# Sparse attention into a gated feed-forward layer: batch 0's last matrix product in seven products, with its neighbours moved

## The chip, the cores and the metric

The kernel runs on one core of one Trainium2 chip. The metric is the device time of one execution in microseconds (us), as the median of several runs. TensorE (PE) does the matmuls, and its weight loads are listed apart as PEld. VectorE (DVE), ScalarE (ACT) and GpSimd (POOL) do the rest of the arithmetic; SyncE (SP), POOL and ACT issue transfers. Each engine works through its own queue in order.

## The reference

```python
def _attn_ref(q, k, v):                  # 4 batches, 8 heads, 768 tokens, 64 per head
    k_sum = k.reshape(B, H, nb, block, D).max(axis=3)        # block = 32, nb = 24
    v_sum = v.reshape(B, H, nb, block, D).mean(axis=3)
    scores_l = scale * q @ k.T           # kept only where |i - j| < 16
    scores_s = scale * q @ k_sum.T + log(block)
    a = softmax(concat([scores_l_masked, scores_s]))
    return a @ concat([v, v_sum])

def _moe_ref(x, w_in, w_out):            # x: 3072 x 512, w_in: 512 x 2048, w_out: 2048 x 512
    h = x @ w_in
    g = h * (1.0 / (1.0 + np.exp(-1.702 * h)))
    return (g @ w_out).astype(np.float32)
```
Each query sees its near neighbours (31 keys at most) and one row for each block of 32: the maximum of the keys, the mean of the values. The result of the attention goes through two matrix products with a gelu between them.

## The kernel before

The four batches run one after the other; a batch's 768 tokens are two halves of 384. The feed-forward layer of one batch runs on PE while the attention of the next batch (or of the same batch's other half, in batch 0) is slipped between its matmuls. All instructions are kept in the order in which the program writes them, on each engine.

Attention of one half, for four pairs of heads p: `scores` (24 narrow matmuls into a two-bank PSUM tile, then an exp on ACT), `mask` (a multiplication on DVE), `values` (48 narrow matmuls for two pairs, then a `norm` on DVE for each), `tx` (six transposes on PE for two pairs and a copy to `xTT`). In batches 2 and 3 a DMA transpose (`dx`) takes the place of `tx`. Before that, queries and keys must stand transposed: batch 0's late queries through `q_late` (PE turn, DVE copy), batch 1's through `tk` and `tq`, those of later batches through the DMA transposes `xk` and `xq`. The rows for the value blocks come from `vsum` (48 narrow matmuls), `block_sums` (DVE) and `sum_dmas`; `halo_dmas` copy the neighbours' rows. `value_rows` is all four.

Feed-forward: an ff tile (`ff_in`, `ff_one`, `ff_open`) is four matmuls of 384 columns into one bank and a gelu on ACT, which writes 128 of the 2048 inner columns of a half into `gT`; 16 tiles make a half. The second product is done in two ways:

- plain (`ff_out`): for a tile of 128 tokens 16 matmuls of 512 columns, in four parts of four. Batch 0 does all six tiles so.
- in seven products (`product`): two tiles of tokens, left and right, and two halves of w_out are combined as in Winograd's form of Strassen's product, so that seven products of eight matmuls with 256 columns give what eight would give otherwise. It needs the sums `ws` of w_out (`w_sum`, once) and the sums `gs` of gT (`g_sums`), and between the products copies (`keep_it`) and additions (`give`) that read the PSUM banks. Batches 1 to 3 do this.

PSUM's eight banks are two pools: `pmm`, four tiles of one bank, and `psb`, two tiles of two banks. A new tile takes the bank that is free first in program order and waits for the last reader of the one before.

What runs between which matmuls is written out by hand: `plan0` (batch 0's second half between its own first half's `ff_out`), `plan1` (batch 1 between batch 0's second `ff_out`), `plan` (batches 2 and 3 between the products of the batch before) and `todo` (work between the second half's ff tiles). An entry such as "s02" means scores, half 0, pair 2; "m" mask, "v" values, "x" turn back, "t" and "q" queries, "d" DMA transpose, "R" the value rows, "g" the gelu table. ACT holds one table at a time, so `exp_soon` and `gelu_soon` load the next one ahead of its first use.

Loads go through POOL's queue in the order of `load_batch`: for batches 1 to 3 keys, values, queries (batch 3's queries later, gated by a small copy that waits for a transfer). Behind them on POOL stand the halo copies of batch 1's keys.

Of the kernel before, what the change touches and what calls it, by code (L numbers as in the profile page):

```python
# [35 lines left out]
def kernel(  # L36
# [295 lines left out]
    def vrows0():  # L332

        dve.tensor_copy(out=gate3[:, 1:2], in_=gate3[:, 0:1])
# [227 lines left out]
    def tq(p, s, eng):  # L562
        ps = pmm.tile([128, 1024], BF16, name="ps_t", tag="mm")[:, 0:S]
# [37 lines left out]
    def values(b, half, g):  # L601

        if b == 1:
# [27 lines left out]
    def tx(half, g):  # L631
        ps = psb.tile([128, 2, HALF], F16, name="ps_x", tag="big")
# [4 lines left out]
        dve.tensor_copy(out=xTT[half][g], in_=ps)  # L637
# [17 lines left out]
    def ff_in(half, nts):  # L655

        phs = [pmm.tile([128, HALF], F32, name="ph", tag="mm") for nt in nts]
# [25 lines left out]
    def g_sums(j, eng=dve, which=(0, 1, 2, 3)):  # L683
# [91 lines left out]
    def product(b, t, what):  # L775
        n = NT // 2
        l = slice(t * 128, t * 128 + 128)
        r = slice(HALF + t * 128, HALF + t * 128 + 128)
        lo, hi = slice(0, N1), slice(N1, d_model)
        raw_l, raw_r = gTb[:, :, l], gTb[:, :, r]  # L780
# [18 lines left out]
        def keep_it(name):  # L799
# [4 lines left out]
            copy(dve if t == 0 and b + 1 < B else act, t_, po)  # L804
# [20 lines left out]
        elif what == 2:  # L825
            give("o1", lo, "s1")
            if last:
                store("o1", t * 128, lo)
# [4 lines left out]
        elif what == 7:  # L833
            give("o2", hi, "s5")
            if last:
                store("o2", HALF + t * 128, hi)
        elif what == 3:
            give("o1", hi, "s2")
            store("o1", t * 128, hi if last else slice(0, d_model))
        elif last:  # L840
            give("o2", lo, None)
            store("o2", HALF + t * 128, lo, act)
        else:
            give("o2", lo, None)
            store("o2", HALF + t * 128)
# [410 lines left out]
```

## Time and profile before

| | |
|---|---|
| median of 3 runs | 206.43 us (206.40 to 206.73) |
| the profiled execution | 205.39 us, its span 203.4 us |
| PE busy | 196.7 us, 97% of the span |
| PEld, DVE, ACT, POOL busy | 136.6, 141.2, 125.4, 89.9 us |
| plain matmuls `po` | 96 |
| matmuls of products in batches 1 to 3 | 504 of 256 columns |
| table loads on ACT | 10 of 1.28 us |
| granted clock of PE | 0.998 of full speed |

The span is the time from the first instruction to the last in the profile. Stages on PE: batch 0's first half of attention up to 20.6 us, its first half's ff tiles up to 30.7, `ff_out` with the second half's attention up to 44.8, the second half's ff tiles up to 57.2, `ff_out` with batch 1's attention up to 74.8, batch 1's ff tiles up to 96.6, its products with batch 2's attention up to 119.0, and the same again for batch 2; batch 3 has no attention beside it. Nearly all instructions are recorded at one line, L28, the wrapper that keeps the order; so they are told apart by the names of their tiles.

### The profile page before, as it was taken

Reading aid. Unit: us, or ns where it says so; the run is one execution under the profiler, and the core shown is the slowest. Engines: PE = TensorE matmul, PEld = TensorE weight load, DVE = VectorE, ACT = ScalarE, POOL = GpSimd, SP = SyncE. Lnnn points to the kernel's source line nnn. Section 1 sums busy time; section 2 is a strip of 40 time slices with the busy share of each in tenths; the row PEclk is TensorE's granted clock in tenths of the full one; section 3 lists DMA queues with packets and bytes.
Section 4 is the critical chain, followed back from the end, with each engine's and each line's share of the span. In section 5 each row is a group of like instructions: output and inputs, shape, how many; then the busy total and the mean of one; then the engine's idle time right before and its main releaser. Section 6 shows DMA issues by size and latency. Waiting matters only on the chain.

```text
span 203.4 us, 5851 instructions
## 1 busy us (share of the span) xinstructions
PE 196.7 (97%) x2358; PEld 136.6 (67%) x2358; DVE 141.2 (69%) x391; ACT 125.4 (62%) x240; POOL 89.9 (44%) x141
## 2 busy tenths in 40 slices
PE   6889999999999999999999999999999999999993
PEld 5548655556754566655888876666888865578882
DVE  6586894694856884898767789896769567758221
ACT  4584976638786717777871446778670559984220
POOL 7964489447899584000986034000000009980000
PEclk9999999999999999999999999999999999999999
DMA  5999999999999999999999979999022930000223
GB/s 171 169 165 204 207 207 215 189 156 243 116 122 170 176 170 178 127 165 155 114 181 156 173 140 139 110 247 179 0 104 62 185 119 3 0 0 0 106 105 103
DMA packets 95994, 28.13 MB, mean 138 GB/s; under 512 B 83664, under 2 KB 93152, under 8 KB 95968
## 3 DMA queue, kind: packets, MB, share of 16 engines
q0 software_dynamic: 69648, 13.24, 84.8%
q1 hardware_dynamic: 26176, 14.39, 34.8%
q8 instruction: 18, 0.29, 0.6%
q10 hardware_dynamic: 144, 0.13, 0.2%
q14 instruction: 8, 0.07, 0.1%
HBM read 27.26 MB, written 6.29 MB: 165 GB/s over the span
## 4 chain that ended last, share of the span: by engine, by line
PE 91%; DMA 3%; DVE 3%; issue 1%; ACT 0%; POOLq 0%; DVEq 0%
PE ph L28 32%; PE poA L28 16%; PE po L28 11%; PE poB L28 7%; PE phA L28 4%; PE ps_av L28 4%; PE poC L28 4%; PE ps_s L28 3%; DMA qe<-in_q_dram 3%; DVE ks L28 2%; PE ps_t L28 1%; PE ps_x L28 1%; PE phC L28 1%; PE phB L28 1%; PE phE L28 1%; DVE qT L28 1%
## 5 line engine op out<-in xcount | busy, mean ns | idle before, releaser
L28 PE MATMUL ph<-xT,w_in_sb 128*128 128x384 f16 x400 | 67.8, 326 | 0.1
L28 PEld LDWEIGHTS <-w_in_sb 128*128 128x128 f16 x442 | 42.7, 98 | 27.2 <-issue 0.2
L28 ACT ACTIVATE gT<-ph 128x384 f16<-128x384 f32 x100 | 47.9, 491 | 18.4 <-PE ph L28 17.6
L28 PEld LDWEIGHTS <-gT 128*128 128x128 f16 x312 | 28.8, 98 | 11.3 <-issue 0.2
L28 ACT ACTIVATE a_sb<-ps_s 128x768 bf16<-128x768 f32 (+1 forms) x32 | 25.0, 826 | 12.0 <-PE ps_s L28 12.0
L28 PEld LDWEIGHTS <-gs 128*128 128x128 f16 x288 | 27.7, 98 | 3.4
L28 POOL DMA_DIRECT2D vw<-in_v_dram x36 | 24.6, 699 | 11.9 <-DMA kb<-in_k_dram 5.4
L28 POOL TENSOR_TENSOR gs<-gT 128x384 f16<-128x384 f16 x8 | 7.3, 911 | 43.3 <-ACT gT L28 43.2
L28 PE MATMUL po<-w_out_sb,gT 128*128 128x512 f16 x96 | 23.6, 380 | 0.0
L28 PE MATMUL poA<-ws,gs 128*128 128x256 f16 x144 | 18.7, 273 | 0.0
L28 DVE TENSOR_TENSOR a_sb<-a_sb,mk 128x768 bf16<-128x768 bf16 x28 | 14.9, 554 | 5.5 <-ACT a_sb L28 5.0
L28 DVE TENSOR_TENSOR x<-ps_av,rc 128x384 f16<-128x384 f32 x32 | 17.8, 557 | 1.1
L28 DVE TENSOR_TENSOR gs<-gT 128x384 f16<-128x384 f16 (+1 forms) x34 | 13.3, 390 | 7.2 <-ACT gT L28 6.9
L28 POOL DMA_DIRECT2D qb<-in_q_dram x16 | 15.1, 961 | 2.5 <-DMA w_in_sb<-in_moe_w_in_dram 1.2
L28 PEld LDWEIGHTS <-kx 64*128 64x128 bf16 (+1 forms) x378 | 9.9, 95 | 6.8 <-issue 3.6
L28 POOL DMA_DIRECT2D kb<-in_k_dram x14 | 13.6, 986 | 0.3 <-issue 0.3
L28 DVE TENSOR_REDUCE ks<-kx 128x24 bf16<-128x768 bf16 x12 | 11.4, 948 | 3.4 <-ACT kx L28 3.2
L28 ACT ACT_TABLE_LOAD x10 | 12.8, 1283 | 1.0 <-PEq L1240 0.8
L28 ACT ACTIVATE osb<-poA 128x256 f32<-128x256 f32 x9 | 3.5, 384 | 16.1 <-PE poA L28 16.1
L28 ACT ACTIVATE s<-poA 128x256 f32<-128x256 f32 x11 | 4.2, 385 | 11.2 <-PE poA L28 11.2
L28 PEld LDWEIGHTS <-a_sb 128*64 128x64 bf16 (+2 forms) x400 | 7.9, 108 | 2.8 <-issue 1.3
L28 PE MATMUL poA<-ws,gT 128*128 128x256 f16 x72 | 9.3, 273 | 0.0
(117 smaller groups left out, 288.2 us busy)
## 6 DMA issues: line engine op xcount, KB each, us to landing
out_dram<-osb SPq DMA_DIRECT2D x22, 256.0 KB, 3.9
kb<-in_k_dram POOLq DMA_DIRECT2D x14, 192.0 KB, 6.6
qb<-in_q_dram POOLq DMA_DIRECT2D x12, 192.0 KB, 10.5
vw<-in_v_dram POOLq DMA_DIRECT2D x36, 64.0 KB, 5.5
w_out_sb<-in_moe_w_out_dram POOLq DMA_DIRECT2D x4, 512.0 KB, 12.8
w_in_sb<-in_moe_w_in_dram POOLq DMA_DIRECT2D x3, 512.0 KB, 12.4
vw<-vs SPq DMA_DIRECT2D x6, 198.0 KB, 6.6
gT<-in_k_dram SPq DMA_DIRECT2D x2, 384.0 KB, 3.4
```

Source lines behind the costliest of these rows:

```text
L28: r = f(*a, **kw)
```

## The change

Batch 0 does two tiles plainly (tokens 0 to 255) and the other four in two groups of seven products (`seq0`), with the left tile of a group in columns 256 and 512 of gT and the right one 128 further. Of the two plain tiles three quarters stand between the second half's attention, and the last quarter behind the first four ff tiles of the second half, which take two banks of each pool. The two groups of products stand where the second half's `ff_out` stood, with batch 1's attention between them.

With that: two of batch 0's late query loads are issued ahead of the first quarter of w_out, and two of the late query turns stand ahead of the last ff tile; batch 0's block rows (`vrows0`) come ahead of the key work; all sums of w_out stand together at the start of the second half's ff tiles; new sums over gT (`g_sums0`, four inner tiles and 256 columns at a time) between and behind these tiles; batch 1's value rows go behind product (0,2). The turns back go through ACT, and most of them through one-bank tiles. Masks 2 and 3 of batch 0's second half stand between two norms. In batch 0's products the copies of group 0 go through ACT. In batches 1 and 2 the matmuls over the next batch's value rows stand behind the last ff tiles and the block sums behind product (0,1); batch 2's queries are loaded ahead of its values, batch 3's queries with its keys and its values later; the query transposes are issued at the third pair of ff tiles in both.

```diff
     def load_batch(b):
...
+        load_turned(q, b, qb2, "qb", (0,) if b == 1 else (0, 1))
+        if b < 3:
+            load_v(b)
         if b == 1:
-            load_turned(q, b, qb2, "qb", (0,))
-        load_v(b)
-        if b < 3:
-            load_turned(q, b, qb2, "qb", (1,) if b == 1 else (0, 1))
+            load_turned(q, b, qb2, "qb", (1,))
...
     def vsum(s):
-        if s == 1 and not vs_ps[0]:
-            ps = [pmm.tile([128, 512], F32, name="ps_vs", tag="mm") for e in range(2)]
-        else:
-            big = psb.tile([128, 1024], F32, name="ps_vs", tag="big")
-            ps = [big[:, 0:512], big[:, 512:1024]]
+        ps = [pmm.tile([128, 512], F32, name="ps_vs", tag="mm") for e in range(2)]
...
     def vrows0():
-        dve.tensor_copy(out=gate3[:, 1:2], in_=gate3[:, 0:1])
...
-    def values(b, half, g):
+    def values(b, half, g, mm=False, between=()):
...
             norm(...)
+            if i == 0:
+                for p in between:
+                    mask(half, p)
...
-    def tx(half, g):
+    def tx(half, g, eng=dve, mm=False):
...
-        dve.tensor_copy(out=xTT[half][g], in_=ps)
+        copy(eng, xTT[half][g], ps)
...
+    def g_sums0(j0, j1, which, eng=dve):
+        def pairs(n0):
+            a = gTb[:, n0 + j0:n0 + j1, HALF - 128:S].rearrange("p j (a i c) -> p j a i c", i=2, c=128)
+            return a[:, :, :, 0], a[:, :, :, 1]
+        (l1, r1), (l2, r2) = pairs(0), pairs(NT // 2)
+        o = [gs[:, w, j0:j1, 0:256].rearrange("p j (a c) -> p j a c", c=128) for w in range(4)]
+        for w in which:
+            a, b_, op = {0: (r1, r2, ALU.add), 1: (o[0], l1, ALU.subtract),
+                         2: (l1, r1, ALU.subtract), 3: (l2, o[1], ALU.subtract)}[w]
+            eng.tensor_tensor(out=o[w], in0=a, in1=b_, op=op)
...
     def product(b, t, what):
-        r = slice(HALF + t * 128, HALF + t * 128 + 128)
+        tok_l, tok_r = (t * 128, HALF + t * 128) if b else (HALF - 128 + t * 256, HALF + t * 256)
...
-            copy(dve if t == 0 and b + 1 < B else act, t_, po)
+            copy(dve if t == 0 and 0 < b and b + 1 < B else act, t_, po)
...
+    seq0 = [(0, 1), (0, 2), (0, 5), (1, 1), (0, 6), (0, 7), (0, 3), (0, 4),
+            (1, 2), (1, 5), (1, 6), (1, 7), (1, 3), (1, 4)]
...
+    for a in range(2):
+        load_q1(a)
     load_w_out(0)
-    for a in range(NP):
+    for a in range(2, NP):
         load_q1(a)
...
     halo_dmas(w50, JH)
+    vrows0()
...
-    plan0 = {1: ["q0", "q1", "q2"], 2: ["s0", "s1", "q3", "m0", "m1"], 4: ["s2", "s3", "m2", "m3"], 6: ["v0", "v1"], 8: ["x0"], 9: ["x1"]}
-    plan1 = {-1: ["s00", "s01"], 1: ["t2", "m00", "m01"], 2: ["t3", "s02"], 3: ["s03", "m02"], 4: ["m03", "s10"],
-             5: ["s11", "m10"], 6: ["v00", "m11", "s12", "s13"], 7: ["v01", "g"], 8: ["m12", "m13"],
-             9: ["x00", "x01", "v10"], 10: ["v11"], 11: ["x10"]}
+    plan0 = {-1: ["s0", "s1"], 0: ["q2"], 1: ["m0", "q3", "m1", "s2", "s3", "v0"],
+             3: ["v1", "x0"], 5: ["x1"]}
+    plan1 = {1: ["R"], 2: ["s00", "s01"], 4: ["t2", "t3", "m00", "m01"], 5: ["s10", "s11"],
+             6: ["m10", "m11"], 7: ["s02", "s03"], 8: ["m02", "m03"], 9: ["s12", "s13"],
+             10: ["m12", "v00", "g"], 11: ["v01"], 12: ["x00", "v10"], 13: ["x01", "v11"]}
...
     for nt in range(N0, NT):
         ff_in(0, (nt,))
-        if nt == 12:
-            act.activation(out=gate3[:, 0:1], in_=gate[:, 0:1], func=ACT.Copy)
-            vrows0()
+        if nt == 14:
+            for p in range(2):
+                q_late(p, dve)
...
-    for i, (ms, part) in enumerate((ms, part) for part in range(4) for ms in range(JH)):
+    for i, (ms, part) in enumerate((ms, part) for part in range(3) for ms in range(2)):
         ff_out(0, ms, part)
         beside0(i)
...
-    ff_in(1, range(3))
-    for nt in range(3, NT):
-        ff_in(1, (nt,))
+    for what, part in ((0, 0), (0, 1), (1, 0), (1, 1), (2, 0), (2, 1), (3, 0), (3, 1)):
+        w_sum(what, part)
...
+    ff_in(1, order2[0:4], 2)
+    for ms in range(2):
+        ff_out(0, ms, 3)
...
-    beside(1, -1)
-    for i, (ms, part) in enumerate((ms, part) for ms in range(JH) for part in range(4)):
-        ff_out(1, ms, part)
+    for i, (t, what) in enumerate(seq0):
+        product(0, t, what)
+        if i == 0:
+            g_sums0(4, NT // 2, (0, 1))
+        if i == 2:
+            g_sums0(4, NT // 2, (2, 3))
         beside(1, i)
-        if i == 2:
+        if i == 4:
             load_batch(2)
...
             if n == 0:
-                ff_open(order2[0:4], (lambda: tx(1, 1)) if b == 1 else None)
+                ff_open(order2[0:4], (lambda: tx(1, 0, act)) if b == 1 else None)
+                if b == 1:
+                    tx(1, 1)
+                    for nt in order2[4:6]:
+                        ff_one(0, nt)
...
                 if n == 0 and b > 1:
-                    load_turned(q, b + 1, qb2, "qb")
-                if n // 2 == 1:
-                    value_rows(s)
-                if n // 2 == 2 * b:
+                    load_v(b + 1)
+                if n // 2 == 7:
+                    halo_dmas(vw[s].rearrange("p (j e) h c -> p j e h c", e=2), 0)
+                    vsum(s)
+                if n // 2 == 2:
                     xq(0, s)
                     xq(1, s)
...
             product(b, t, what)
             if i == 0:
+                if nxt:
+                    block_sums()
+                    sum_dmas(vw[s].rearrange("p (j e) h c -> p j e h c", e=2), 0)
                 g_sums(NT // 2 - 1, dve, (2, 3))
```

More of the change, by code (lines that the diff above doesn't have):

```diff
@@ L560, in tk, with tq @@
         rest_k(p, s, pool)
-    def tq(p, s, eng):
-        ps = pmm.tile([128, 1024], BF16, name="ps_t", tag="mm")[:, 0:S]
+    def tq(p, s, eng, big=False):
+        ps = (psb.tile([128, 2048], BF16, name="ps_t", tag="big") if big
+              else pmm.tile([128, 1024], BF16, name="ps_t", tag="mm"))[:, 0:S]
         turn_tiles(ps, qb2[p // 2][:, p % 2], NJ)
@@ L629, in norm @@
                        rc.to_broadcast([128, 2, JH, D]))
-    def tx(half, g):
-        ps = psb.tile([128, 2, HALF], F16, name="ps_x", tag="big")
+    def tx(half, g, eng=dve, mm=False):
+        ps = (pmm if mm else psb).tile([128, 2, HALF], F16, name="ps_x", tag="mm" if mm else "big")
         for i in range(2):
@@ L653, in ff_step, with ff_in @@
                       rhs=xTT[half][g][:, i], start=(n == 0), stop=(n == KO - 1))
-    def ff_in(half, nts):
-        phs = [pmm.tile([128, HALF], F32, name="ph", tag="mm") for nt in nts]
+    def ff_in(half, nts, n_mm=4):
+        phs = [pmm.tile([128, HALF], F32, name="ph", tag="mm") if i < n_mm
+               else psb.tile([128, 1024], F32, name="ph", tag="big")[:, 0:HALF] for i in range(len(nts))]
         for part in ((0, 1), (2, 3)):
@@ L827, in product @@
             if last:
-                store("o1", t * 128, lo)
+                store("o1", tok_l, lo)
         elif what == 6:
@@ L1051, in beside0 @@
             elif what[0] == "v":
-                values(0, 1, i)
+                values(0, 1, i, i == 0, (2, 3) if i == 0 else ())
             else:
-                tx(1, i)
+                tx(1, i, act)
     def beside(b, slot):
@@ L1059, in beside @@
             if what[0] == "t":
-                tq(i, 1, dve)
+                tq(i, 1, dve, True)
             elif what[0] == "m":
@@ L1069, in beside @@
             elif what[0] == "v":
-                values(b, half, i)
+                first_ = b == 1 and half == i == 0
+                values(b, half, i, first_)
+                if first_:
+                    mask(1, 3)
             elif what[0] == "d":
@@ L1073, in beside @@
             else:
-                tx(half, i)
+                tx(half, i, act, True)
     def value_rows(s):
@@ L1138 @@
                 for nt in order2[n:n + 2]:
-                    for half in range(2):
+                    for half in range(int(b == 1 and n == 4), 2):
                         ff_one(half, nt)
```

33 lines of the change are left out of this document (17 added, 16 removed).

## The prediction

> **What bounds the kernel now.** I read the page first, then the busy time of each engine in the stages that the change touches, then the chain of waits in order of time.
>
> ```profile
> span 203.4 us, 5851 instructions
> ...
> PE 196.7 (97%) x2358; PEld 136.6 (67%) x2358; DVE 141.2 (69%) x391; ACT 125.4 (62%) x240; POOL 89.9 (44%) x141
> ...
> PE 91%; DMA 3%; DVE 3%; issue 1%; ACT 0%; POOLq 0%; DVEq 0%
> ```
> ```profile
> core 0: us, PE busy (x) PEld busy (x) DVE busy (x) ACT busy (x) POOL busy (x), PEclk, DMA share, GB/s
> 30.66:44.83 14.17, 14.17 (x183) 7.42 (x181) 9.16 (x21) 7.68 (x11) 9.18 (x12) 1.00 1.80 188
> ...
> 57.23:74.79 17.56, 17.56 (x320) 9.95 (x320) 12.73 (x33) 10.89 (x16) 14.36 (x23) 1.00 1.78 160
> ...
> 96.56:118.97 22.41, 22.41 (x362) 19.28 (x361) 15.65 (x41) 12.16 (x21) 12.28 (x17) 1.00 1.55 161
> ```
> The chain is TensorE's for 91%. In the two stretches where batch 0 leaves through w_out (30.66 to 44.83, with its own second half's attention, and 57.23 to 74.79, with batch 1's), and in batch 1's (96.56 to 118.97), PE is busy all the time at the full granted clock. So the kernel is a row of matmuls without gaps: what the change takes from that row is won, and every wait that it opens is lost. VectorE and ScalarE have slack on average; what counts is who is late at one place.
>
> **What the matmuls cost.** Chain of waits; each piece runs from the end of the one before to its own end:
>
> ```profile
> 19.73 0.04 issue
> 19.77 0.48 PE ph L28 x2
> ```
> ```profile
> 20.59 10.07 PE ph L28 x62
> ...
> 32.39 0.62 PE ps_q L28 x18
> ...
> 34.44 0.29 PE ps_q L28 x6
> ...
> 38.85 0.88 PE ps_av L28 x48
> ...
> 41.56 0.34 PE ps_x L28 x6
> ...
> 43.10 1.73 PE po L28 x8
> ...
> 57.23 0.53 PE ps_vs L28 x48
> 57.77 0.46 PE ps_s L28 x24
> ...
> 61.59 0.28 PE ps_s L28 x12
> 61.87 0.97 PE po L28 x4
> ...
> 71.52 0.50 PE ps_av L28 x24
> ...
> 98.00 0.87 PE poB L28 x8
> ```
> A plain matmul of 512 columns takes 1.73/8 = 0.216 us, a product (eight matmuls of 256 columns) 0.873, shown as 0.87. Four plain matmuls are 0.86; behind scores they are 0.97, so each step from narrow tiles to full ones costs 0.11. An ff tile is 4 x 0.162 = 0.65.
>
> Removed: 64 plain matmuls, 13.84 us. Added: 14 products, 14 x 0.873 = 12.22. Saved 1.62. The narrow work stays the same in number but is grouped otherwise: values in six groups of 24 (3.00) instead of 0.88 + 4 x 0.50 (+0.12), four single scores of 0.28 become two pairs of 0.46 (-0.20), one more step to full tiles (+0.11), the late queries in three groups instead of two (+0.13): +0.16. The sum over the value rows of batches 2 and 3 moves to where scores and not ff tiles follow it: 2 x -0.11. Together PE has 1.68 us less to do, if it never waits.
>
> [...]
>
> **What PE will wait for.** A stall costs more than the lateness: in the row at 19.77, PE starts 0.04 after ScalarE's end, and two matmuls take 0.48 instead of 2 x 0.162. So I let a released group end 0.21 us later than its release plus its own length (0.04 and 0.16, rounded up). Timeline, then groups by form:
>
> ```profile
> 29.55 1.11 DVE L28 COPY vs<-vs 24x128 bf16<-24x128 bf16 x4
> ...
> 32.72 1.49 DVE L28 COPY qT<-ps_q 128x384 bf16<-128x384 bf16 x3 [2.06 <-PE ps_q L28]
> ```
> ```profile
> 57.27 0.49 ACT L28 ACTIVATE gT<-ph 128x384 f16<-128x384 f32 x1 [0.16 <-PE ph L28]
> ...
> 57.78 1.28 ACT L28 ACT_TABLE_LOAD   x1
> ...
> 59.18 1.50 ACT L28 ACTIVATE a_sb<-ps_s 128x768 bf16<-128x768 f32 x2
> ```
> ```profile
> L28 DVE TENSOR_TENSOR x<-ps_av,rc 128x384 f16<-128x384 f32 x32 | 17.8, 557 | 1.1
> ...
> L28 DVE TENSOR_TENSOR a_sb<-a_sb,mk 128x768 bf16<-128x768 bf16 x28 | 14.9, 554 | 5.5 <-ACT a_sb L28 5.0
> ...
> L28 DVE TENSOR_TENSOR gs<-gT 128x384 f16<-128x384 f16 x33 | 11.7, 355 | 7.2 <-ACT gT L28 6.9
> ...
> L28 DVE RECIPROCAL rc<-ps_av 128x6 f32<-128x6 f32 x32 | 6.0, 188 | 2.9 <-PE ps_av L28 2.6
> ...
> L28 ACT ACTIVATE s<-poA 128x256 f32<-128x256 f32 x11 | 4.2, 385 | 11.2 <-PE poA L28 11.2
> ...
> L28 DVE TENSOR_TENSOR vs<-ps_vs,vpart 32x128 bf16<-32x128 f32 x12 | 3.4, 284 | 0.2
> ...
> L28 ACT ACTIVATE kx<-ps_t 128x768 bf16<-128x768 bf16 x4 | 3.2, 804 | 0.0
> ...
> L28 DVE TENSOR_TENSOR ws<-w_out_sb 128x1024 f16<-128x1024 f16 x4 | 2.6, 682 | 0.0
> L28 DVE TENSOR_TENSOR osb<-poC,s 128x256 f32<-128x256 f32 x6 | 2.5, 423 | 3.9 <-PE poC L28 3.9
> ```
> The load starts 0.02 after the last gelu's end, the first exp 1.40 after the load's start. Three query copies take 1.49, not 3 x 0.55: neighbours on VectorE overlap by about 0.08.
>
> *Batch 0, second half* (on the clock of the trace before). Six groups of plain matmuls are left as cover, where twelve stood. The ff tile before the last ends at 30.01 (30.66 less 0.65); two query turns (0.46) and a step (0.11) stand ahead of the last, which ends at 31.22. VectorE is free at about 30.5: the block rows that ended at 30.66 now come ahead of the key work, which ends that much later, and a small copy that gated them is gone. Query copies end at 31.06 and 31.53; scores 1 need the second: 31.53 + 0.21 + 0.23 = 31.98, 0.25 late. Then plain, turn, plain, turn, scores 2, to 34.75. ScalarE's gelu, load and two exps end at 33.97 and 34.66. VectorE does mask 0 to 34.55, the fourth query copy to 35.09, mask 1 to 35.52. Scores 3 need that copy, with scores 2 alone as cover: 35.09 + 0.21 + 0.23 = 35.54 instead of 34.98, 0.56 late. First values to 36.04, two plain groups to 37.87, second values to 38.37. The first turn back needs a norm (0.19 + 0.56) that stands behind masks 2 and 3 and ends at 38.33: 0.17 late. Two plain groups, the second turn; its copy, now ScalarE's (0.80 as in the kx row), ends at 41.79 and holds the PSUM of the fourth ff tile 0.08 too long. Sum 1.06. Bounds: 0.2 more or less at each place.
>
> *ff tiles of the second half.* ScalarE has 16 gelus of 0.49, four key copies of 0.80 and two evictions in some 14 us of PE; the eight sums of w_out (0.68 each, gathered here) and the new sums over gT lie in VectorE's idle time. I cost these at nothing; if ScalarE ran 1 us behind, all of it would show at the end of this stretch.
>
> *Batch 0's products.* Counted from the end of the last ff tile: its gelu ends at 0.53, ScalarE goes on at 1.95 behind the exp load, has product (0,1) copied by 2.33, VectorE has (0,2) added by 2.79, and only that frees the bank of (0,5). PE has (0,1), (0,2) and the value sums before it, 2.27. So (0,5) ends at 2.79 + 0.21 + 0.87 = 3.87 instead of 3.25: 0.62 late. Its new sum over gT (1024 columns; between the 0.36 of 384 and the 0.68 of a w_out sum of the same size, I take the latter) is done at 1.3, its second at 1.9: hidden. Product (1,7) waits for ScalarE's copy of (1,6), queued behind a copy and two exps after (1,5): 0.04 + 0.39 + 1.50 + 0.39 = 2.3, against scores, (1,6) and values on PE, 1.94: 0.46 late. Sum 1.08. The tail (four turns, three on ScalarE) is covered by products and by two more ff tiles of the first half.
>
> *Batches 1 and 2.* The value sums now lie in matmul banks at the end of the ff tiles, and a copy and four adds for the block rows (5 x 0.28) stand on VectorE between the copies of (0,1) and of (0,5) and (0,6), with two gs sums. With the overlaps, the copy of (0,6) ends 5.11 after the last ff tile, so (0,7) ends at 6.19 instead of 6.02: 0.17 late, in two batches 0.34.
>
> [...]
>
> Transfers moved (issues by line in a stretch, a tile's landings at 58 to 62 and 83 to 85, and the page's store row):
>
> ```profile
> w_out_sb<-in_moe_w_out_dram POOLq DMA_DIRECT2D x1, 512.0 KB, 15.3
> ```
> ```profile
> DMA to landing us min/median/max: 4.7/5.1/5.6
> ```
> ```profile
> DMA to landing us min/median/max: 9.8/9.9/10.0
> ```
> ```profile
> out_dram<-osb SPq DMA_DIRECT2D x22, 256.0 KB, 3.9
> ```
> The first quarter of w_out, issued at about 13.6, lands at 28.9; behind two query loads of 96 KB some 1 us later, still 2 us before its use at 32.0. The two landing rows are the block rows of batches 1 and 2. For batch 2 they are now issued about 4.5 us after the ff tiles and needed at 12.6: hidden at 5.6. A third output tile back must be stored before its buffer is written again, 6.4 us here: hidden at 3.9. On GpSimd's queue batch 2's queries pass its values, and batch 3's values take the place of its queries; on SP's, the query transposes pass the halo rows. All have most of an ff stretch (21 us): nothing.
>
> **Sum.** Waits 1.06 + 1.08 + 0.34 = 2.48, less 1.68 saved: +0.80. The profiled execution took 205.39 us (2.0 more than its span) and becomes 206.2; the median of the three is 206.43, which becomes 207.2.
>
> **Rivals.** 0.2% (0.41 us) is about what a measurement of this kernel can tell from no change.
>
> *Faster: a restart costs only the hand-over.* If a waiting PE's first matmul costs no extra 0.16, the eight places give 0.08 + 0.39 + 0 + 0 + 0.45 + 0.29 + 0 + 0 = 1.21, and the net is -0.47: 205.9 at the median. It decides where a restart costs under 0.05. The row at 19.77 speaks against it; that it is one place, with two matmuls alone, speaks for it. 0.20.
>
> *Even.* At 0.12 a restart the waits come to about 1.7, the saving: 206.4. A VectorE that packs its queue closer does the same. 0.20.
>
> *Slower still: late block rows.* If batch 2's rows take 10.0 to land, they come at 14.5 and hold the values 1.9 us: 208.9 with the other waits. Key and query loads run beside them, as at 59.5, not transposes, which speaks against. 0.11.
>
> *Short matmuls dearer.* If each added product paid the step of 0.11, 1.5 us of the saving were gone: 208.7. The row at 98.00 shows 0.87 in a stream; 0.02. [...]
>
> [...]
>
> That the early query loads do nothing is likely enough, as the old ones landed in time; the sum has nothing for them.
>
> **Numbers.** Forecast 207.2, chance 0.46. Faster 0.20, same 0.20, slower 0.46 + 0.11 + 0.02 + 0.01 = 0.60. The range goes from 205.7 (restart free, VectorE ready 0.2 sooner) to 208.7 (each of the eight places 0.19 later than worked out).
>
> **What would show it.** In the chain after, VectorE and ScalarE appear between 31 and 42 and between 55 and 72: before the fourth scores of batch 0 (from a qT copy), before poB of (0,5) (from osb), before (1,7) (from s). The first ff tiles of batch 1 would start near 75.1, not 74.8. I am wrong if these gaps sum to under half, if ff tiles of the second half wait for gT, or if batch 2's values wait for vw.

## The result, and the profile after

The changed kernel took 208.46 us (median of 15 runs) against 206.40 (15 runs): a ratio of 1.0089, 95% interval 1.0061 to 1.0117, or 1.3 to 2.4 us more. A second set on another chip gave 1.0117 (1.0070 to 1.0164). Forecast were 0.8 us more. Medians here and below take in every execution; ratios and spreads leave out the few that fell in a slower state. The profiled execution took 208.06 us, its span 206.1.

The page of the changed kernel, with the span, PE's line and the chain by engine:

```profile
span 206.1 us, 5961 instructions
...
PE 197.8 (96%) x2406; PEld 143.3 (70%) x2406; DVE 145.9 (71%) x399; ACT 128.9 (63%) x248; POOL 93.3 (45%) x141
...
PE 61%; DMA 18%; POOL 11%; issue 3%; DVE 2%; ACT 2%; SPq 0%; POOLq 0%; DVEq 0%
```
TensorE no longer carries 91% of the chain but 61%, and 29% are transfers and GpSimd. That is the first sign that something other than a late VectorE is at work. PE's own busy time is no measure here: it went from 196.7 to 197.8 though there is less work, because an early stage, whose matmuls the change does not touch, ran slower in this execution. Timeline of PE, before and then after:

```profile
6.14 0.53 PE L28 MATMUL ps_k<-wide,kb 128*64 128x128 bf16 x12
...
19.77 0.48 PE L28 MATMUL ph<-xT,w_in_sb 128*128 128x384 f16 x2
```
```profile
7.18 0.85 PE L28 MATMUL ps_k<-wide,kb 128*64 128x128 bf16 x12
...
20.57 0.48 PE L28 MATMUL ph<-xT,w_in_sb 128*128 128x384 f16 x2
```
The same twelve narrow matmuls take 0.85 instead of 0.53, and the first ff tile starts 0.80 later. In the other runs below it starts anywhere from 18.83 to 19.85. So I compare profiles from the start of the first ff tile to the end of the span: 183.6 us before, 185.5 after, 1.9 more. Of the 2.7 by which the spans differ, 0.8 lies ahead of it.

Behind that point the timeline of PE shows every place where it waits; the bracket holds the idle time and what ended it:

```profile
32.02 0.82 PE L28 MATMUL ps_s<-qT,kx 64*128 64x64 bf16 x24
32.77 1.04 PE L28 MATMUL po<-w_out_sb,gT 128*128 128x512 f16 x4
...
35.28 0.35 PE L28 MATMUL ps_s<-qT,kx 64*128 64x64 bf16 x12
36.01 0.35 PE L28 MATMUL ps_s<-qT,kx 64*128 64x64 bf16 x12 [0.38 <-DVE qT L28]
36.29 0.57 PE L28 MATMUL ps_av<-vw,a_sb 128*64 128x65 bf16 x24
...
53.80 2.11 PE L28 MATMUL ph<-xT,w_in_sb 128*128 128x384 f16 x12
...
57.59 0.60 PE L28 MATMUL ps_vs<-vw,E 64*32 64x128 bf16 x48
58.74 1.03 PE L28 MATMUL poB<-ws,gs 128*128 128x256 f16 x8 [0.55 <-DVE osb L28]
59.70 0.52 PE L28 MATMUL ps_s<-qT,kx 64*128 64x64 bf16 x24
60.16 1.05 PE L28 MATMUL poA<-w_out_sb,gT 128*128 128x256 f16 x8
61.05 1.04 PE L28 MATMUL poA<-ws,gs 128*128 128x256 f16 x8
...
69.61 0.57 PE L28 MATMUL ps_av<-vw,a_sb 128*64 128x65 bf16 x24
70.45 1.03 PE L28 MATMUL poA<-ws,gs 128*128 128x256 f16 x8 [0.27 <-ACT s L28]
71.41 0.57 PE L28 MATMUL ps_av<-vw,a_sb 128*64 128x65 bf16 x24
```
```profile
100.86 1.04 PE L28 MATMUL poC<-w_out_sb,gT 128*128 128x256 f16 x8
101.83 0.52 PE L28 MATMUL ps_s<-qT,kx 64*128 64x64 bf16 x24
102.65 1.03 PE L28 MATMUL poA<-ws,gs 128*128 128x256 f16 x8 [0.30 <-DVE s L28]
103.52 1.04 PE L28 MATMUL poB<-w_out_sb,gs 128*128 128x256 f16 x8
...
109.98 0.22 PE L28 MATMUL ps_av<-vw,a_sb 128*64 128x65 bf16 x1
111.12 0.92 PE L28 MATMUL ps_av<-vw,a_sb 128*64 128x65 bf16 x47 [0.92 <-DMA vw<-vs]
111.97 1.05 PE L28 MATMUL poA<-ws,gs 128*128 128x256 f16 x8
...
148.01 1.03 PE L28 MATMUL poA<-ws,gs 128*128 128x256 f16 x8 [0.29 <-DVE s L28]
```
All but one are the places that the prediction named. The other is at 111.12: one matmul of batch 2's first values runs at 109.98, the next waits 0.92 for the block rows. From 109.98 to 111.97 are 1.99 us where such values take 0.88, so this place costs 1.11. The block rows' tile in the changed kernel, 100.9 to 102 us (issue times on SyncE's queue, then landing):

```profile
L28 SPq DMA_DIRECT2D vw<-vs x2: 585/593/601, 101.2 to 101.8; - x2
...
DMA to landing us min/median/max: 8.1/8.6/9.2
```
They took 8.1 and 9.2 us; the prediction had them hidden at 5.6. Behind them stands a longer chain. GpSimd's loads of batch 2's values from 60 to 95 us, before and then after (first and last issue, then the time to landing):

```profile
L28 POOL DMA_DIRECT2D vw<-in_v_dram x12: 679/698/758, 62.9 to 73.6; - x12
...
DMA to landing us min/median/max: 5.3/6.6/8.4
```
```profile
L28 POOL DMA_DIRECT2D vw<-in_v_dram x12: 677/679/799, 67.5 to 86.9; - x12
...
DMA to landing us min/median/max: 9.2/12.5/16.4
```
In both kernels batch 2's loads begin near 59 (58.9 and 59.5). With the queries ahead of them the twelve value loads are issued up to 86.9 instead of 73.6 and take 9.2 to 16.4 us each. The last one takes 9.3 and so lands at 96.2; the value sums that read it start at 97.2. The changed kernel has 1 us to spare there, then the halo copies, the block sums, the block rows.

### The profile page after: what moved, and what is told of

Its sections match the earlier page's. It is cut to its first block, busy times and chain, and to the rows that moved or that the text cites. A ratio compares the mean times of both kernels' runs of the same rounds, so it can differ in the third digit from the quotient of the medians.

```text
span 206.1 us, 5961 instructions
## 1 busy us (share of the span) xinstructions
PE 197.8 (96%) x2406; PEld 143.3 (70%) x2406; DVE 145.9 (71%) x399; ACT 128.9 (63%) x248; POOL 93.3 (45%) x141
## 4 chain that ended last, share of the span: by engine, by line
PE 61%; DMA 18%; POOL 11%; issue 3%; DVE 2%; ACT 2%; SPq 0%; POOLq 0%; DVEq 0%
PE ph L28 21%; PE poA L28 16%; DMA qb<-in_q_dram 8%; PE poB L28 8%; DMA w_in_sb<-in_moe_w_in_dram 6%; DMA vw<-vs 4%; PE phA L28 4%; PE poC L28 3%; POOL mk L28 3%; PE ps_av L28 2%; POOL kb L28 2%; POOL v0n L28 2%; PE ps_s L28 2%; POOL vw L28 1%; PE phC L28 1%
## 5 line engine op out<-in xcount | busy, mean ns | idle before, releaser
L28 PEld LDWEIGHTS <-gs 128*128 128x128 f16 x352 | 33.8, 98 | 5.6 <-issue 1.3
L28 PEld LDWEIGHTS <-gT 128*128 128x128 f16 x296 | 27.9, 98 | 6.6
L28 PE MATMUL poA<-ws,gs 128*128 128x256 f16 x176 | 22.8, 273 | 0.9 <-DVE s L28 0.6
L28 DVE TENSOR_TENSOR gs<-gT 128x384 f16<-128x384 f16 (+2 forms) x38 | 16.1, 424 | 8.1 <-ACT gT L28 7.7
L28 ACT ACTIVATE osb<-poA 128x256 f32<-128x256 f32 x11 | 4.2, 383 | 17.0 <-PE poA L28 17.0
L28 ACT ACTIVATE s<-poA 128x256 f32<-128x256 f32 x15 | 5.8, 385 | 12.6 <-PE poA L28 12.6
L28 PE MATMUL poB<-ws,gs 128*128 128x256 f16 x88 | 11.4, 273 | 0.5 <-DVE osb L28 0.5
L28 PE MATMUL poA<-w_out_sb,gT 128*128 128x256 f16 x88 | 11.5, 273 | 0.0
L28 PE MATMUL poA<-ws,gT 128*128 128x256 f16 x88 | 11.4, 273 | 0.0
```

The source lines that it names most:

```text
L28: r = f(*a, **kw)
```

## The experiments

Twelve kernels in three groups (e1 to e4, e5 to e8, e9 to e12), each group on a chip of its own together with the kernel before. Each ratio is to the kernel before on the same chip, with its 95% interval; medians of different groups are not compared. "From ff" is the span less the start of the first ff tile in the one profiled execution, and its difference to the 183.6 of before; it holds for that execution alone.

| run | what | median us | ratio | first ff tile | from ff |
|---|---|---|---|---|---|
| (after) | the change | 208.46 | 1.0089 (1.0061 to 1.0117) | 20.57 | 185.5, +1.9 |
| e11 | the change again | 207.87 | 1.0117 (1.0070 to 1.0164) | 19.64 | 186.1, +2.5 |
| e1 | change, rows and loads back | 207.94 | 1.0114 (1.0063 to 1.0165) | 19.06 | 188.4, +4.8 |
| e2 | before, rows and loads moved | 206.32 | 1.0013 (0.9981 to 1.0045) | 19.59 | 184.9, +1.3 |
| e3 | change, batch 3's queries late | 207.50 | 1.0071 (1.0035 to 1.0108) | 19.85 | 184.4, +0.8 |
| e4 | change, three waits removed | 208.20 | 1.0093 (1.0058 to 1.0129) | 18.83 | 186.9, +3.3 |
| e5 | e3 and e4 together | 208.35 | 1.0085 (1.0046 to 1.0124) | 19.08 | 185.2, +1.6 |
| e6 | e5, batch 2's query loads left out | 205.87 | 0.9997 (0.9967 to 1.0027) | 19.34 | 184.2, +0.6 |
| e7 | e5, values between the queries | 207.99 | 1.0087 (1.0045 to 1.0128) | 19.45 | 186.2, +2.6 |
| e8 | before, batch 2's query loads left out | 205.56 | 0.9986 (0.9962 to 1.0009) | 19.68 | 184.0, +0.4 |
| e9 | change, batch 2's query loads left out | 205.38 | 0.9997 (0.9970 to 1.0023) | 19.11 | 184.5, +0.9 |
| e10 | e6 and all waits treated | 204.05 | 0.9920 (0.9889 to 0.9952) | 19.20 | 182.9, -0.7 |
| e12 | all work done, eight value loads early | 205.75 | 1.0008 (0.9985 to 1.0031) | 19.08 | 184.4, +0.8 |

My theory at first (A): the change loses what it showed, simple waits behind a named instruction, and the block rows are slow only because of the loads beside them.

**e1: the value rows back.** In batches 1 and 2 the rows stand at the second pair of ff tiles again, and batch 2's values ahead of its queries:

```diff
-                if n // 2 == 7:
-                    halo_dmas(vw[s].rearrange("p (j e) h c -> p j e h c", e=2), 0)
-                    vsum(s)
+                if n // 2 == 1:
+                    value_rows(s)
```


> The changed kernel with the value rows of batches 2 and 3 (halo copies, sums, block sums, block rows) and the loads of batches 2 and 3 put back where they stood before; batch 0's seven products stay. Theory A (the late rows cost most of the loss): the wait of batch 2's values for the block rows (0.92 us idle and the restart, 1.1 in all) and the two waits of product (0,7) (0.3 each) are gone, the narrow sums go back between ff tiles (+0.1 twice): 1.4 to 1.5 us less than the changed kernel, so 0.3 to 0.5 more than the kernel before. In its chain no piece of vw<-vs stands ahead of batch 2's values, and (0,7) of batches 1 and 2 follows without idle time. Theory B (the late rows come from what batch 0's edits do to the timing of the loads, not from where the rows stand): the rows or the halo copies still hold PE somewhere in batch 1, and less than 0.7 us is won.

Measured: 1.0114, no better than the change. Timeline of PE:

```profile
82.82 0.21 PE L28 MATMUL ps_vs<-vw,E 64*32 64x128 bf16 x1 [0.83 <-DMA vw<-in_v_dram]
84.62 0.25 PE L28 MATMUL ps_vs<-vw,E 64*32 64x128 bf16 x7 [1.59 <-DMA vw<-in_v_dram]
...
144.87 0.53 PE L28 MATMUL ps_s<-qT,kx 64*128 64x64 bf16 x24 [1.59 <-DMA qT<-qb]
```
The wait at the block rows is gone, but now PE waits 2.4 us for the loaded values themselves and later 1.6 for a query transpose. The last value load is issued at 75.4 and lands at 84.6, where the kernel before had it at 80.0 and asked for it at 80.3. PE comes to that place no sooner than before (81.5 against 80.3); it is the loads that come later. Their order is that of the kernel before, but they begin at 60.5 instead of 58.9, since GpSimd's copies of batch 1's keys ahead of them take 6.5 us instead of 4.2, and the value loads then take 7.1 to 9.3 to land instead of 5.3 to 8.4. Which of batch 0's edits does this was not tested. The profiled execution took 209.52, four of the six 207.8 to 208.0; so its 4.8 are more than usual. Putting the rows back wins nothing: Theory A fails, and B is nearer. Moving the rows gave the loads more time.

**e2: the rows alone.** The other half on the kernel before:

```diff
+                if n // 2 == 7:
+                    halo_dmas(...)
+                    vsum(s)
```


> The kernel before with only the other half of the change: value sums behind the last ff tiles and block sums behind product (0,1) in batches 1 and 2, batch 2's queries ahead of its values, batch 3's queries with its keys and its values later, query transposes at the third pair of ff tiles. Batch 0 is as before. Theory A: the block rows of batch 2 land 8 to 9 us after their issue, batch 2's values wait about 1 us for them, and (0,7) waits 0.3 in two batches: 1.2 to 1.5 us more than the kernel before. Theory B (the rows are late only with batch 0's edits): they land within 6 us, no wait for vw, 0 to 0.4 us more.

```profile
109.38 0.92 PE L28 MATMUL ps_av<-vw,a_sb 128*64 128x65 bf16 x47 [0.42 <-DMA vw<-vs]
```
The block rows landed late (8.5 and 8.7 us) and (0,7) waited 0.3 twice, as by A, but the wait for the rows was only 0.42. They were issued as long ahead of their use as in the change (8.4 us for the second), and the second took 8.7 instead of 9.2. The time, 1.0013 or 0.3 us more, is what B forecast (0 to 0.4), though the places are those of A and the profiled execution is 1.3 longer from the first ff tile. The losses of the two halves, 1.0114 and 1.0013, do not tell which of them is to blame: one half alone, batch 0's, loses as much as both.

**e3: batch 3's queries behind the block rows.**

```diff
+                    pool.tensor_copy(out=gate2[0:32], in_=vw[s][0:32, NQ - 1, 0, 0:1])
+                    load_turned(q, b + 2, qb2, "qb")
```


> The changed kernel with one load moved: batch 3's four query loads (192 KB each) start only when the block rows of batch 2 have landed, through a small copy on GpSimd that reads one of these rows. Theory A (the query loads beside the block rows make these slow): the two transfers of block rows land in 6 us or less instead of 8.1 and 9.2, the values of batch 2 do not wait, 0.9 to 1.2 us less than the changed kernel. Theory C (the rows are slow because of the halo copies and key loads ahead of them, or because of their own form): they still take over 7.5 us, and the time changes by less than 0.3. In between: each a part. The query transposes come 30 us later and should not notice.

```profile
DMA to landing us min/median/max: 5.0/5.1/5.1
```
The rows land in 5.0 and 5.1 us, and in this execution PE waits for no transfer; from the first ff tile it is 0.8 above before, the very sum of the prediction. So the query loads beside the rows make these slow, as A has it. But the median, 207.50, is well above this execution's 206.37: other executions lose about 1 us more somewhere. (Those of before spread as well, from 204.7 to 207.4.)

**e4: three waits of batch 0 removed.**

```diff
-    plan0 = {..., 1: ["m0", "q3", "m1", ...
+    plan0 = {..., 1: ["q3", "m0", "m1", ...
-    exp_soon()
     for i, (t, what) in enumerate(seq0):
         product(0, t, what)
         if i == 0:
+            exp_soon()
...
+            copy(dve if t == 0 and 0 < b and b + 1 < B or (b, t, name) == (0, 1, "s2") else act, t_, po)
```


> The changed kernel with the three largest waits of batch 0 taken away, each by what makes it wait: the fourth late query's copy stands ahead of mask 0 on VectorE (scores 3 waited 0.45); the exp table is loaded behind ScalarE's copy of product (0,1) instead of ahead of it (product (0,5) waited 0.6); the copy of product (1,6) is VectorE's (product (1,7) waited 0.35). Theory A (these are simple waits behind one named instruction): all three idle times are gone and nothing takes their place, 1.2 to 1.5 us less than the changed kernel, the first ff tiles of batch 1 start that much sooner. Theory D (engines are so full there that the next wait is just behind): one or two of the places wait again, first values behind mask 1, the exps of batch 1 behind the table load, or values 0 behind a mask, and less than 0.7 us is won.

Measured: 1.0093, nothing won. Timeline of PE:

```profile
56.87 1.03 PE L28 MATMUL poB<-ws,gs 128*128 128x256 f16 x8 [0.15 <-DVE osb L28]
...
95.86 0.25 PE L28 MATMUL ps_vs<-vw,E 64*32 64x128 bf16 x7 [0.40 <-DMA vw<-in_v_dram]
...
97.07 0.25 PE L28 MATMUL ps_vs<-vw,E 64*32 64x128 bf16 x7 [0.44 <-DMA vw<-in_v_dram]
...
109.77 0.19 PE L28 MATMUL ps_av<-vw,a_sb 128*64 128x65 bf16 x1 [0.25 <-DMA vw<-vs]
110.66 0.92 PE L28 MATMUL ps_av<-vw,a_sb 128*64 128x65 bf16 x47 [0.69 <-DMA vw<-vs]
```
(0,5) waits 0.15 instead of 0.55 and (1,7) not at all; scores 3 still waits 0.38, since the turn itself still stands right ahead of scores 2 on PE, whose 0.28 do not cover the copy (0.56). What was won is given back at 95.9 to 97.1, where PE waits for batch 2's values, and at 110.7. The rows end their wait at 110.66, after at 111.12: with a first ff tile 1.74 sooner and waits removed, PE is 0.46 ahead there.

This made a second theory (L): the loads go through GpSimd's queue at a pace of their own, batch 2's arrive near 96 and its block rows near 110 whatever PE does ahead, and what PE saves in batch 0 it waits there. e5 to e8 test it.

**e5: e3 and e4 together.**

> The two edits put together: batch 3's query loads behind the block rows of batch 2, and the exp table, the copy of (1,6) and the fourth late query's copy as in the run without waits. Theory A (simple waits, each worth what it shows): PE gains 0.4 + 0.3 on the kernel with late queries alone, counted from the first ff tile to the end. Theory L (GpSimd's queue of loads has a clock of its own, and batch 2's values land near 96 whatever PE does): batch 2's value sums then wait for vw<-in_v_dram as in the run without waits (0.4 + 0.3 + 0.4 us idle) and nothing is gained on the kernel with late queries alone; the time stays within 0.4 of it.

```profile
96.81 0.25 PE L28 MATMUL ps_vs<-vw,E 64*32 64x128 bf16 x7 [0.68 <-DMA vw<-in_v_dram]
```
By L: 1.0085, not better than e3, and PE waits 0.68 for the values, up to nearly the same time as in e4 (96.8 against 97.1). Its executions spread from 206.31 to 209.18.

**e6: the same without batch 2's query loads.**

```diff
-        if b < 3:
-            load_turned(q, b, qb2, "qb", (0,) if b == 1 else (0, 1))
+        if b == 1:
+            load_turned(q, b, qb2, "qb", (0,))
```


> The same kernel without batch 2's four query loads: batch 2 computes with batch 1's queries, all other work is there. Theory L: batch 2's values land near 80 instead of 96, no wait for a transfer is left on PE in batches 1 and 2, and the whole, counted from the first ff tile, comes 0.2 to 0.9 below the kernel before (1.46 saved on PE, less what is left of the waits: 0.4 and 0.15 in batch 0, 0.3 twice at (0,7), each with its restart). Theory A: the loads did not bind, so it stays where the run with both edits is.

0.9997, where e5 stood at 1.0085. No wait for a transfer is left. L holds and A does not. Scores 3 wait 0.38, though, (0,5) 0.35 and (0,7) still 0.30 twice, so it comes level with before, not below, as L had it.

**e8: the control.** The same loads left out of the kernel before.

> The control: the kernel before without batch 2's four query loads (batch 2 computes with batch 1's queries). PE does not wait for a transfer there, so by both theories its time stays: within 0.3% of the kernel before, no idle time on PE behind the first ff tile. If it gets faster by more, the loads cost the kernel before something, too, and the run without these loads must be compared with this one.

0.9986 (0.9962 to 1.0009): these loads cost the kernel before nothing that can be told. One wait opened (0.33 for a query transpose of batch 3), which I had not expected.

**e7: another order of the loads.** Values between the halves of the queries, batch 3's keys behind the second query transpose, and two more fixes:

```diff
+            load_turned(q, b, qb2, "qb", (0,))
             load_v(b)
-        if b == 1:
             load_turned(q, b, qb2, "qb", (1,))
...
-    0: ["q2"], 1: ["q3", "m0", ...
+    0: ["q2", "q3"], 1: ["m0", ...
...
+            copy(dve if t == 0 and 0 < b and b + 1 < B and name != "s2" or (b, t, name) == (0, 1, "s2") else act, t_, po)
```


> The run with both edits, and batch 2's values between the two halves of its queries instead of behind both, the second query transpose behind the halo copies, batch 3's keys behind that; besides, the fourth query turn right behind the third (its copy had only scores 2 as cover), and the copy of (0,6) in batches 1 and 2 on ScalarE, which is idle there ((0,7) waited 0.3). Theory L: values land by 92, the block rows by 106, the second half of qT by 100, all before PE asks; no wait for a transfer, none at scores 3 and (0,7); 0.5 to 1.2 below the kernel before, counted from the first ff tile. If the loads are too slow even so, PE waits at batch 2's third scores for qT or at its value sums for vw, and it comes out level or slower.

```profile
100.46 0.52 PE L28 MATMUL ps_s<-qT,kx 64*128 64x64 bf16 x24 [0.77 <-DMA qT<-qb]
120.05 1.03 PE L28 MATMUL poA<-ws,gT 128*128 128x256 f16 x8 [1.89 <-DVE osb L28]
```
A miss: 1.0087. Values and block rows came in time (92.5 and 102.9), but now the second half of the queries is late at 100.46, and at 120.05 PE waits 1.89 for VectorE's osb. Here moving a load only moved the wait. The copy of (0,6) on ScalarE did take the wait at (0,7) away.

**e9: the change itself without batch 2's query loads.**

```diff
-        load_turned(q, b, qb2, "qb", (0,) if b == 1 else (0, 1))
+        if b != 2:
+            load_turned(q, b, qb2, "qb", (0,) if b == 1 else (0, 1))
```


> The changed kernel, all its waits in it, without batch 2's four query loads (batch 2 computes with batch 1's queries). Theory L (what the change loses beyond its working is that PE now asks for batch 2's transfers at the moment when the chain of loads delivers them): values land near 83, the block rows by 106, no wait for a transfer; left is the working's 0.8, so 0.3 to 0.5% above the kernel before instead of 0.9, about 1 us less than the changed kernel. Theory A (the block rows are slow only because of batch 3's query loads beside them, which are still there): the values of batch 2 still wait 0.6 us or more for vw<-vs, and the time stays within 0.3% of the changed kernel.

The value loads, and then the block rows:

```profile
DMA to landing us min/median/max: 7.0/8.2/9.7
```
```profile
DMA to landing us min/median/max: 5.3/5.4/5.5
```
0.9997: by the medians the whole loss is gone, with every wait of batch 0 and (0,7) still there. The last value load lands at 84.4 (96.2 in the change), the rows at 105.6, and batch 3's query loads, which still come, are through by 104.7. From the first ff tile it is 0.9 above before, near the 0.8 of the working; the median is lower than that, because the first ff tile stands at 19.1 and not 19.8 and only 1.7 us instead of 2.0 lie outside the span (205.27 against 203.6). Against e11, on the same chip, the profiled execution is 2.3 us shorter: 1.6 of it lie behind the start of the first ff tile, and only these can be put down to the loads.

**e10: the loads light and all waits treated.** e6 with the two further edits of e7 at scores 3 and (0,7).

> The run without batch 2's query loads, with batch 3's late and the waits of batch 0 treated, and two more edits: the fourth query turn right behind the third, and the copy of (0,6) in batches 1 and 2 on ScalarE. So the waits at scores 3, (0,5), (1,7) and (0,7) are all taken away, and the loads are light. If the saving on PE is as worked out (1.5 to 1.7), it shows here: 0.3 to 0.9 us below the control (the kernel before without these loads), counted from the first ff tile, up to 0.4% below the kernel before. If it stays level with the control, the products cost PE more than 0.87 each in their places, and the saving was never there.

```profile
56.87 1.03 PE L28 MATMUL poB<-ws,gs 128*128 128x256 f16 x8 [0.35 <-DVE osb L28]
```
That is the only wait left on PE behind the first ff tile. 0.9920 (0.9889 to 0.9952), 1.1 us under the control from the first ff tile: more than I expected. If each matmul is given the time to the start of the next one, the plain matmuls and products together take 79.55 us here and 81.41 before. So the saving on PE is real. Here it is had with four loads left out; with all loads it was not reached.

**e11: the change again.**

> The changed kernel itself, on the chip of the other runs. By theory L its wait for the block rows depends on where the prologue happens to leave PE against the loads: a profile that reaches the first ff tile sooner than 20.57 us shows more idle time ahead of batch 2's values (or its value sums), one that reaches it later shows less, with these transfers landing at about the same time (96 and 109 to 111). By theory A the wait is the same 0.9 at any prologue, since the block rows follow PE. 0.6 to 1.1% above the kernel before by both.

```profile
110.39 0.92 PE L28 MATMUL ps_av<-vw,a_sb 128*64 128x65 bf16 x47 [0.90 <-DMA vw<-vs]
```
With a first ff tile 0.93 sooner the wait for the rows is 0.24 + 0.90 instead of 0.92, and it ends 0.73 sooner. That is between the theories: the rows are issued by PE's progress (100.2 instead of 101.2) and took 9.0 and 9.4 us. For the rows alone A and L cannot be parted; for the values ahead of them e4 and e5 part them, and e9 shows what the whole chain costs.

**e12: the change without its waits, all work done.** As e10, with batch 2's queries, and:

```diff
+    todo = {..., 5: [lambda: tk(1, 1, act), lambda: load_v(2, range(4))],
...
+            load_v(b, range(4 if b == 2 else 0, NJ))
...
+                if n == 0 and b == 1:
+                    xk(0, 0)
+                    xk(1, 0)
```


> A try at the change without its waits, all work done: as the run with both edits, with the two further edits at scores 3 and (0,7), and eight of batch 2's twelve value loads issued ahead of GpSimd's work on batch 1's third and fourth pair of keys, when the transfers have little to do; batch 2's key transposes go behind the products of batch 0. Theory L: values land by 92, PE does not wait for them, and PE's saving shows from the first ff tile to the end: level with the kernel before or up to 0.8 us below it. Against it: GpSimd ends the keys of pairs 2 and 3 of batch 1 some 5 us later (about 64 to 65, their scores stand near 64 to 65), and batch 2's keys and queries land later; then PE waits there, and it is slower.

```profile
65.49 0.35 PE L28 MATMUL ps_s<-qT,kx 64*128 64x64 bf16 x12 [1.02 <-POOL kx L28]
```
1.0008 (0.9985 to 1.0031): level with before, and 2.1 us under the change on the same chip (205.75 against 207.87). No wait for a transfer is left, and the rows land in 2.7 and 3.3 us. The price is the one that was feared: batch 1's fourth scores wait 1.02 for GpSimd's keys, which stand behind the early loads. It does not beat the kernel before. A version that does all the work and is below it was not found. By e10 at most about 1.6 us would be to be had if batch 2's loads came sooner without holding the keys; that is not shown.

## Why the prediction was right in direction and short in size

The forecast was 207.2, slower by 0.8; measured were 1.3 to 2.4 more. The range (to 208.7) and the side were right, the likeliest case was not: it held up to 97 us and missed what comes behind. That 208.46 lies in the range is in part luck. Its upper end stood for each of eight places 0.19 later; what came was one wait of 1.11 at a ninth place, which the sum had at nothing. Of the three signs of being wrong that the prediction named, one came: batch 2's values waited for vw.

- **PE's saving, 1.68.** Nearly right. In the changed kernel itself plain matmuls and products, each given the time to the start of the next, take 1.8 less (1.62 forecast). In e10 they take 1.86 less; from the first ff tile 0.7 are left of it, since (0,5) and scores 1 still wait (0.4 and 0.3) and the narrow groups take 0.4 more. Without these two waits it would be 1.4.
- **A restart costs 0.21.** The 0.16 in it was misread: it is no price of waiting. A group is listed up to the end of its last matmul, and that lies behind the start that a next one would have, waiting or not: (0,5), which waited, is listed with 1.03, the product at 60.16, which did not, with 1.05, and there the next starts after 0.89. The prediction counts from end to end, so the 0.16 stands on both sides, and its times come out: (0,5) ends 3.86 behind the last ff tile (59.77 against 55.91), 3.87 was forecast. From start to start a restart costs nothing: (0,7) starts 0.36 later than its scores allow (102.65 against 101.83 + 0.46), and the place costs 0.34 in all.
- **Batch 0, second half, 1.06.** Scores 1: 32.02 to 32.77 instead of 0.46, 0.29 (0.25 forecast). Scores 2 and 3: 35.28 to 36.29 instead of 0.56, 0.45 (0.56), ended by the named copy of qT. The first turn back did not wait (0.17); the fourth tile did, by 0.09 (0.08). Sum 0.83.
- **ff tiles of the second half, nothing.** Right: no wait of PE is listed between 36.3 and 58.7.
- **Batch 0's products, 1.08.** (0,5) waits for osb behind the exp load: 57.59 to 59.70 is 2.11, where the sums take 0.53 and a product ahead of narrow matmuls 0.97 (100.86 to 101.83), so 0.61 (0.62). (1,7) waits for ScalarE's copy: 1.80 less 0.50 + 0.97, 0.33 (0.46).
- **(0,7) in batches 1 and 2, 0.17 each.** Under-sized: from 101.83 to 103.52 are 1.69, where scores and product take 0.46 + 0.89 (as at 59.70 to 61.05), so 0.34. The place and the instruction were right; VectorE's copy of (0,6) ends 5.28 behind the last ff tile (102.59 against 97.31), where 5.11 was worked out.
- **Transfers moved: nothing.** This is the step that failed. The prediction took the shorter of two landing times for the block rows because "Key and query loads run beside them, as at 59.5, not transposes". At 59.5 only key and value loads were beside them. The rows of 9.8 and 10.0 stood beside three query loads, issued at 75.3 to 77.3 and landed at 86.2, 92.2 and 94.1, though beside key transposes and halo copies as well. e3 shows that just the query loads make them slow (9.2 against 5.0). That is the rival "late block rows", which had 0.11 (its time, by the prediction's own sum, is 207.2 + 1.9 = 209.1, not 208.9). It did take in what GpSimd's queue is moved past, but asked only whether each transfer had time enough, not whether the whole chain of loads, from 59 us on, still ran ahead of PE. From the first ff tile to the end, e9 shows this to be the whole of the loss beyond the working.

Without that step: 0.29 + 0.45 + 0.09 + 0.61 + 0.33 + 2 x 0.34 = 2.45 of waits less 1.68 are 0.77, and from the first ff tile e3 is 0.8 above before and e9 0.9. With 1.11 for the block rows it makes 1.9, as the changed kernel's profile shows.

The rival "faster, a restart costs only the hand-over" had its premise right and its sum wrong: it took 0.16 away from each place on one side alone. No short matmul was dearer: 60.16 to 61.05 is 0.89, behind scores. No run shows the dearer table load that the last 0.01 of the chances stands for: the load takes 1.28, ScalarE goes on 1.42 after the last gelu's end as in the kernel before (57.86 against 56.44), and (0,5), which stands behind it, is 0.61 late, where 0.62 was worked out.

What stays open: why the first ff tile starts between 18.83 and 20.57 us in executions of the same instructions, and whether the new order of the early loads has a part in it (19.59 to 19.77 in the three profiles with the old order, 19.2 in the middle of eleven with the new). In e9's profile it is worth 0.7 us against that of before. Open, too, is why batch 0's edits let GpSimd's loads begin later (e1), and what e3's longer executions wait for; e5's profile, with a wait of 0.68 for the same values, suggests the loads, but no profile of such an execution of e3 was taken.

## What to carry to other kernels

A kernel whose PE is busy for 97% can still have its loads land only just in time: look when each load lands and when it is asked for, and count that slack (0.3 us in the kernel before, 80.0 against 80.3) as the most that a saving ahead of it can bring while the loads stay as they are: what e4 won in batch 0 it waited for at 96 and 110 us. Leaving out the loads of one tensor is a cheap way to see whether a change lost its gain to the transfers. And when the price of a moved transfer has two rows, 5.6 and 10.0, take what runs beside it at the new place as the question to settle, not as a reason for the lower one.

## What the runs showed of the hardware

GpSimd's loads in this program stop at eight in flight: in the traces of before and after, with 81 loads each, no more are seen, and each one from the ninth on is issued 0.28 us or more after the load eight places ahead of it has landed. The chain in the changed kernel, GpSimd's timeline:

```profile
63.54 4.08 POOL L28 DMA_DIRECT2D qb<-in_q_dram  x4
67.53 1.45 POOL L28 DMA_DIRECT2D vw<-in_v_dram  x2
69.23 0.68 POOL L28 DMA_DIRECT2D vw<-in_v_dram  x1 [0.25 <-DMA kb<-in_k_dram]
...
74.10 0.68 POOL L28 DMA_DIRECT2D vw<-in_v_dram  x1 [3.16 <-DMA qb<-in_q_dram]
77.98 0.68 POOL L28 DMA_DIRECT2D vw<-in_v_dram  x1 [3.20 <-DMA qb<-in_q_dram]
```
From 59.53 on four key loads, four query loads and two value loads go out, then each of the next six value loads waits for a key or query load to land, twice 3.2 us behind the 192 KB of a query load. So the four query loads put ahead of the value loads of 64 KB held places of the queue, and GpSimd waited 7.8 us in all for them. Whether the limit is the chip's or the program's these runs do not tell.

The block rows, two transfers of 198 KB on SyncE's queue, landed in 2.7 to 3.3 us in e10 and e12 and in 5.0 to 5.1 in e3, in all of which batch 3's query loads stand behind them; in 5.3 to 5.5 in e9, where these loads are through by 104.7; and in 8.1 to 9.4 beside four query loads on GpSimd's queue (after, e11). So the same transfers took about three times as long there as in e12.

In the slow early stage of the changed kernel's profile, the twelve narrow matmuls are listed with 1.6 times the time of before (0.85 against 0.53) and follow each other at near half the pace (a pair each 0.107 us against 0.056), while the clock's column shows 1.00 in both from 4.9 to 10.3 us. What slows this stage no run shows, so the cause stays open.
